# One zero region of the value-cache gradient: from one SyncE store to two GpSimd stores of eight rows

## The chip, the cores and the metric

The kernel runs on one core of a Trainium2 chip. A core has five engines that work side by side: TensorE (PE, and PEld for its weight loads), VectorE (DVE), ScalarE (ACT), GpSimd (POOL) and SyncE (SP), which here only issues transfers. Transfers between the device memory and the core's on-chip memory are carried out by 16 DMA engines that the issuing engines share. The metric is the device time of one execution in microseconds.

## The reference

The reference is the forward pass and the gradients of one decode step of a transformer block: attention over the last part of a key and value cache, beside a gated feed-forward layer, both on the normalised input.

```python
W = min(4096, max(256, Sk // 4))                    # Sk = 4096, so W = 1024
k = jnp.repeat(k_cache[:, :, Sk - W:, :], rep, axis=1)
v = jnp.repeat(v_cache[:, :, Sk - W:, :], rep, axis=1)
scores = jnp.einsum("bhqd,bhkd->bhqk", q, k) * (Dh ** -0.5)
p = _softmax(scores, axis=-1)
o = jnp.einsum("bhqk,bhkd->bhqd", p, v)
...
return x + _A_ref(xn, A_k_cache, A_v_cache, A_wq, A_wo) + _B_ref(xn, B_w_gate, B_w_up, B_w_down)
...
_out, _vjp = jax.vjp(_f, A_x, A_k_cache, A_v_cache, A_wq, A_wo, B_w_gate, B_w_up, B_w_down)
```

The batch is 4, with one query position each, a model width of 512, 32 query heads on 8 key heads of 128, and a hidden width of 1792. All tensors are bfloat16. Nine outputs are returned: the result and eight gradients. The gradients of the two caches have the caches' full shape, 4 x 8 x 4096 x 128. Only the last 1024 positions of each head were used, so the first 3072 positions of both gradients are zero, and the kernel has to write these zeros: 2 caches x 4 x 8 x 3072 x 128 x 2 bytes, which is most of what it stores.

## The kernel before

The program goes through four stages. First the weights are loaded and the feed-forward layer is computed with its gradients. Then follows the preparation of the attention (queries, and the gradient of the attention's output through `wo`). Then there is a loop over the four batch rows, in which each turn computes the scores, the softmax and its gradient, and the gradients of the used part of the two caches, four stores of 1 MB per turn. The last phase computes the gradients of `wo` and `wq` (eight results of 1 MB) and the two small outputs.

Large results are copied from the accumulators into a stage of four buffers (`stg`) and stored from there by SyncE. The engines' orders, GpSimd's apart, are as written. Loads and stores go through SyncE's queue in program order, with the exception of one small input.

The zeros are written from one tile, `ztile` (L215 to L217), whose partitions hold 6144 zeros (12 KB) each. A zero region is two heads' 3072 positions of one batch row of one cache gradient. There are 32 regions of 1536 KB, listed in `ztodo` (L265). `zeros(n)` (L273) takes the next n of them and has SyncE store each one from 64 of the tile's partitions, every second one, in pieces of 12 KB. `zsrc` is that source pattern: 64 rows, each read twice. With `deep=4`, a zero store waits until the fourth one before it has landed.

When the zeros go out is written by hand. `result()` stores a finished result, and before it takes as many zero regions as the list `before` (L105) has for that result. Further zeros follow some loads (`zeros(2)`, `zeros(3)` and others). In the last phase the list was `[2] + [1] * 7`: two regions ahead of the first of the eight weight-gradient results, then one ahead of each.

Around the change, GpSimd clears tiles: `dhs` (L394) in the feed-forward stage, then `bd`, `selh` and `dqs` (L443 to L450) in the preparation. In the loop it copies columns into `bd` (`refill`, L520). It issues no transfer. `wo` is loaded by SyncE at L302, the last of the weight loads. The head of the last phase is at L779 to L785, after the sum `s_o`; there, the last three pieces of the last cache-gradient results (`last`) have still to leave the accumulators in program order, and the latest zero region taken is the third of those ahead of the two previous results.

Of the kernel before, what the change touches and what calls it, by code (L numbers as in the profile page):

```python
# [19 lines left out]
def kernel(  # L20
# [24 lines left out]
    nc = tc.nc  # L45
# [7 lines left out]
    K0 = Sk - W  # L53
# [4 lines left out]
    KH = HD // P  # L58
# [43 lines left out]
    def stg_tile():  # L102
        return stage.tile([P, 4096], BF16, name="stg", tag="stg")

    before = deque([0, 0, 0, 1, 1, 1] + [0, 0, 1, 0] + [0, 0, 2, 0] + [0, 0, 2, 0] + [3, 0, 2, 0] + [2] + [1] * 7)  # L105

    def result(out, in_):
        zeros(min(before.popleft(), len(ztodo)))
# [106 lines left out]
    ZW = K0 // ZP * Dh  # L215
    ztile = const.tile([P, ZW], BF16, name="ztile")
# [32 lines left out]
    wo_sb = wres.tile([P, KH, D], BF16, name="wo_sb")  # L249
# [15 lines left out]
    zsrc = bass.AP(tensor=ztile.tensor, offset=ztile.offset, ap=[[2 * ztile[:].ap[0][0], ZP], [0, ZG], [1, ZW]])  # L265
    ztodo = [(og, b, g) for b in range(B) for g in range(0, G, ZG) for og in (out_2, out_3)]
    zdone = []

    def behind(ins, other):
        tc.add_manual_dep(ins, other.name,  # L270
                          mybir.DependencyInfo(mybir.DependencyClass.Sync, mybir.DependencyReason.DATA))
# [13 lines left out]
    if True:  # L285
# [13 lines left out]
        nc.sync.dma_start(out=wu_sb[:].rearrange("p c f -> p (c f)"), in_=B_w_up.rearrange("(p c) f -> p (c f)", c=C))  # L299
        nc.sync.dma_start(out=wd_sb[:].rearrange("p c n -> p (c n)"), in_=B_w_down.rearrange("(p c) n -> p (c n)", c=FB))  # L300
        nc.sync.dma_start(out=wq_sb[:].rearrange("p c n -> p (c n)"), in_=A_wq.rearrange("(p c) n -> p (c n)", c=C))
        nc.sync.dma_start(out=wo_sb[:].rearrange("p k n -> p (k n)"), in_=A_wo.rearrange("(p k) n -> p (k n)", k=KH))  # L302

        for wsb, t_ in ((wg_sb, hg), (wu_sb, hu)):
            ps = bank("h_ps", "w", (P, FQ))
# [116 lines left out]
    with tc.tile_pool(name="mid", bufs=1, reuse_waits="tile") as mid:  # L422
# [4 lines left out]
        with (tc.tile_pool(name="kvp", bufs=1, reuse_waits="tile") as kvp,  # L427
# [7 lines left out]
            D3 = [att.tile([P, B, DPB, Q], U32, name=n) for n in ("D3q", "D3d")]  # L435
            qm = att.tile([P, B, 4, Dh], BF16, name="qm")
            rows = [qm[:], dyBD[:].rearrange("p n r x -> p (n r x)").rearrange("p (b g d) -> p b g d", b=B, g=4)]
            bd = []
            for k in range(2):
                bd.append([])  # L440
# [120 lines left out]
            def small(name, shape=(P, 1)):  # L561
                return att.tile(list(shape), FP32, name=name, tag=name)
# [77 lines left out]
            for b in range(B):  # L640
                S = sps[0][:]
                m = small("m")
# [136 lines left out]
            s_o = sums[:, 0:D]  # L779
            TT(out=s_o, in0=ob_ps[:], in1=fo[:], op=ALU.add)  # L780

            dwo_v = out_5.rearrange("(p t k) n -> t p (k n)", t=4, k=8)
            dwq_v = out_4.rearrange("(p c) j -> c p j", c=C)
            late = {}
# [126 lines left out]
```

## Time and profile before

| what | value |
|---|---|
| median of 3 runs | 276.7 us (276.59 to 276.91) |
| the profiled execution | 276.85 us |
| its span, first to last instruction | 275.1 us |
| bytes moved | 111.88 MB: HBM read 30.68, written 81.01 |
| mean transfer rate | 407 GB/s |
| busy share PE, PEld, DVE, ACT, POOL | 62, 21, 64, 44, 11% |
| chain that ended last, by engine | PE 27, DVE 17, ACT 7, DMA 6, issue 4% |
| zero stores | 32 of 1536 KB, median 18.3 us from issue to landing |
| mean granted TensorE clock | 0.603 |

The profile page cuts the span into 40 slices of 6.9 us. Each digit of its line "DMA" is the mean busy share of the 16 DMA engines in that slice, in tenths, and the line below gives the rate. Other views list the instructions of an engine in order of time ("start, duration, line, operation, output<-input"; the issue of a transfer is counted with its waiting), busy time by stretch, and the chain of waits that ended last. The trace also has each DMA packet's start, duration and size, and the times at which each transfer's completion semaphore was raised. A packet is one piece of a transfer on one DMA engine; the trace doesn't say on which.

### The profile page before, as it was taken

Reading aid. Unit: us, or ns where it says so; the run is one execution under the profiler, and the core shown is the slowest. Engines: PE = TensorE matmul, PEld = TensorE weight load, DVE = VectorE, ACT = ScalarE, POOL = GpSimd, SP = SyncE. Lnnn points to the kernel's source line nnn. Section 1 sums busy time; section 2 is a strip of 40 time slices with the busy share of each in tenths; the row PEclk is TensorE's granted clock in tenths of the full one; section 3 lists DMA queues with packets and bytes.
Section 4 is the critical chain, followed back from the end, with each engine's and each line's share of the span. In section 5 each row is a group of like instructions: output and inputs, shape, how many; then the busy total and the mean of one; then the engine's idle time right before and its main releaser. Section 6 shows DMA issues by size and latency. Waiting matters only on the chain.

```text
span 275.1 us, 3144 instructions
## 1 busy us (share of the span) xinstructions
PE 171.7 (62%) x1095; PEld 57.4 (21%) x1095; DVE 175.8 (64%) x332; ACT 122.1 (44%) x246; POOL 30.7 (11%) x91
## 2 busy tenths in 40 slices
PE   1257988878247668937788778987979956200000
PEld 0121341123023212313223322341112311000000
DVE  7879669988887497515784498619996688300000
ACT  2343674940202766543675556647574455300000
POOL 8500005251152011200000000000000000000000
PEclk9985885558855955555555555555595575555555
DMA  7999989999999999999999999999999999999993
GB/s 267 435 472 401 434 338 421 429 423 403 425 403 436 407 415 415 409 412 402 406 408 433 400 417 417 429 406 431 418 420 407 417 416 429 423 424 421 421 426 152
DMA packets 24432, 111.88 MB, mean 407 GB/s; under 512 B 1361, under 2 KB 1377, under 8 KB 18785
## 3 DMA queue, kind: packets, MB, share of 16 engines
q1 hardware_dynamic: 24408, 111.69, 99.5%
q8 instruction: 8, 0.13, 0.2%
q14 instruction: 8, 0.06, 0.0%
q10 hardware_dynamic: 8, 0.00, 0.0%
HBM read 30.68 MB, written 81.01 MB: 406 GB/s over the span
## 4 chain that ended last, share of the span: by engine, by line
PE 27%; DVE 17%; ACT 7%; DMA 6%; issue 4%; DVEq 0%; ACTq 0%
DVE scr L94 8%; DMA out_dram<-stg 6%; PE kv_ps L131 5%; PE dw_ps L131 4%; PE od_ps L131 4%; PE sc_ps L131 3%; ACT stg L114 2%; PE ok_ps L131 2%; DVE dqs L728 2%; DVE stg L114 2%; ACT late L114 2%; PE dxq_ps L131 1%; DVE wq_t L94 1%; PE dn_ps L131 1%; PE ob_ps L131 1%
## 5 line engine op out<-in xcount | busy, mean ns | idle before, releaser
L114 ACT CAST stg<-kv_ps 128x512 bf16<-128x512 f32 x102 | 54.6, 601 | 41.0 <-PE kv_ps L131 34.1
L131 PE MATMUL sc_ps<-scr,bd 128*32 128x256 bf16 x256 | 19.6, 399 | 17.1 <-DVE scr L94 16.7
L131 PE MATMUL kv_ps<-qm,spr 64*128 64x512 bf16 x64 | 24.3, 582 | 2.2 <-DVE stg L114 0.8
L131 PE MATMUL kv_ps<-dyBD,spr 64*128 64x512 bf16 x64 | 20.7, 584 | 3.4 <-ACT stg L114 3.3
L94 DVE STREAM_TRANSPOSE scr<-va 128x1024 uint32<-128x1024 uint32 x16 | 19.5, 1224 | 0.0
L114 DVE CAST stg<-kv_ps 128x512 bf16<-128x512 f32 x10 | 6.6, 689 | 16.0 <-PE kv_ps L131 16.0
L131 PEld LDWEIGHTS <-spr 64*128 64x128 bf16 (+1 forms) x192 | 9.2, 106 | 29.4 <-issue 25.0
L612 DVE SCALAR_TENSOR_TENSOR odt<-od_ps,om,odt 128x128 f32<-128x128 f32 x12 | 4.2, 351 | 15.6 <-ACT odt L607 15.4
L131 PEld LDWEIGHTS <-bd 128*32 128x32 bf16 x256 | 6.3, 106 | 34.2 <-issue 33.4
L89 ACT CAST stg<-dwg_ps 128x448 bf16<-128x448 f32 x26 | 11.9, 571 | 3.0 <-DVE scr L94 1.9
L114 DVE CAST stg<-dw_ps 128x512 bf16<-128x512 f32 x16 | 10.5, 685 | 4.2 <-PE dw_ps L131 4.0
L131 PE MATMUL dw_ps<-scr,xn_b 32*128 32x512 bf16 x32 | 9.6, 546 | 5.7 <-ACT late L114 4.0
L114 ACT CAST late<-dw_ps 128x512 bf16<-128x512 f32 x16 | 9.2, 587 | 8.5 <-PE dw_ps L131 8.5
L131 PE MATMUL do_ps<-scr,dyBD 128*128 128x512 bf16 x32 | 10.6, 472 | 2.4 <-DVE scr L94 2.3
L114 DVE CAST late<-dw_ps 128x512 bf16<-128x512 f32 x16 | 10.6, 678 | 1.8 <-PE dw_ps L131 1.7
L114 ACT CAST stg<-dw_ps 128x512 bf16<-128x512 f32 x16 | 8.9, 588 | 5.9 <-PE dw_ps L131 5.3
L94 DVE STREAM_TRANSPOSE scr<-wo_sb 128x1024 uint32<-128x1024 uint32 x8 | 9.7, 1230 | 1.3 <-ACT scr L465 0.7
L94 DVE STREAM_TRANSPOSE scr<-ka 128x1024 uint32<-128x1024 uint32 x8 | 9.8, 1234 | 0.8 <-PE r_ps L131 0.7
L94 DVE STREAM_TRANSPOSE scr<-kb 128x1024 uint32<-128x1024 uint32 x8 | 9.9, 1240 | 0.1
L520 POOL COPY bd<-D3d 32x64 bf16<-32x64 bf16 x32 | 7.0, 231 | 23.7 <-DVE D3d L94 11.4
L520 POOL COPY bd<-D3q 32x64 bf16<-32x64 bf16 x32 | 7.2, 239 | 19.6 <-PE sc_ps L131 15.9
L131 PE MATMUL dw_ps<-dy_b,scr 32*128 32x512 bf16 x32 | 8.5, 528 | 1.0 <-ACT late L114 0.7
(200 smaller groups left out, 314.7 us busy)
## 6 DMA issues: line engine op xcount, KB each, us to landing
out_dram<-ztile SPq DMA_DIRECT2D x32, 1536.0 KB, 18.3
out_dram<-stg SPq DMA_DIRECT2D x18, 1024.0 KB, 16.2
va<-in_A_v_cache_dram SPq DMA_DIRECT2D x8, 1024.0 KB, 12.9
out_dram<-stg SPq DMA_DIRECT2D x6, 896.0 KB, 8.5
wq_sb<-in_A_wq_dram SPq DMA_DIRECT2D x1, 4096.0 KB
wo_sb<-in_A_wo_dram SPq DMA_DIRECT2D x1, 4096.0 KB
ka<-in_A_k_cache_dram SPq DMA_DIRECT2D x4, 1024.0 KB, 12.7
kb<-in_A_k_cache_dram SPq DMA_DIRECT2D x4, 1024.0 KB, 15.6
```

The source lines that it names most:

```text
L89: return nc.scalar.copy(out=out, in_=in_)
L94: nc.vector.transpose(out=out, in_=in_)
L114: return nc.scalar.copy(out=out, in_=in_) if eng == "act" else nc.vector.tensor_copy(out=out, in_=in_)
L131: nc.tensor.matmul(out, lhsT=lhsT, rhs=rhs, start=first, stop=last, **kw)
L520: nc.gpsimd.tensor_copy(out=t_[q, :, :, g2, :, o_:o_ + 4], in_=src[q, b, g2])
L612: STT(out=t_[:], in0=ps[:, g, :], scalar=(om, oms)[k][:, g:g + 1], in1=t_[:], op0=ALU.mult, op1=ALU.add)
L728: nc.vector.tensor_copy(out=dqs[q, :, :, :, a * B + b], in_=d3v[q])
```

## The change

One of the 32 zero regions, the last of the list, is taken out of `ztodo`: heads 6 and 7 of batch row 3 of the value cache's gradient. SyncE no longer stores it, and the list `before` has one region ahead of each of the eight last results. GpSimd stores it in two halves, one head each. Each half has 8 rows with 8 pieces of 12 KB: the source is eight partitions of `ztile` (0, 2, ... 14), each read eight times, and the target's 3072 positions are cut into 8 x 8 runs of 48.

The first half stands in the program ahead of GpSimd's clearing of `bd` and waits until the load of `wo` has landed. The second stands at the head of the last phase and waits for the zero store that SyncE took last before that place.

```diff
-    before = deque([0, 0, 0, 1, 1, 1] + [0, 0, 1, 0] + [0, 0, 2, 0] + [0, 0, 2, 0] + [3, 0, 2, 0] + [2] + [1] * 7)
+    before = deque([0, 0, 0, 1, 1, 1] + [0, 0, 1, 0] + [0, 0, 2, 0] + [0, 0, 2, 0] + [3, 0, 2, 0] + [1] * 8)
...
     zdone = []
+    zog, zb, zg = ztodo.pop()
+
+    def half_zeros(h, after):
+
+        z = nc.gpsimd.dma_start(
+            out=zog[zb, zg + h, 0:K0, :].rearrange("(m i j) d -> m i (j d)", m=8, i=8),
+            in_=bass.AP(tensor=ztile.tensor, offset=ztile.offset, ap=[[2 * ztile[:].ap[0][0], 8], [0, 8], [1, ZW]]))
+        behind(z.ins, after.ins)
...
-        nc.sync.dma_start(out=wo_sb[:].rearrange("p k n -> p (k n)"), in_=A_wo.rearrange("(p k) n -> p (k n)", k=KH))
+        wo_d = nc.sync.dma_start(out=wo_sb[:].rearrange("p k n -> p (k n)"),
+                                 in_=A_wo.rearrange("(p k) n -> p (k n)", k=KH))
...
+            half_zeros(0, wo_d)
             bd = []
...
             TT(out=s_o, in0=ob_ps[:], in1=fo[:], op=ALU.add)
 
+            half_zeros(1, zdone[-1])
             dwo_v = out_5.rearrange("(p t k) n -> t p (k n)", t=4, k=8)
```

## The prediction

> **What bounds the kernel now.** I read the transfer lines of the page first, since every one of their slices is full:
>
> ```profile
> DMA  7999989999999999999999999999999999999993
> GB/s 267 435 472 401 434 338 421 429 423 403 425 403 436 407 415 415 409 412 402 406 408 433 400 417 417 429 406 431 418 420 407 417 416 429 423 424 421 421 426 152
> ...
> q1 hardware_dynamic: 24408, 111.69, 99.5%
> ```
>
> The 16 DMA engines are busy from the first slice to the last, and nearly all of it is one queue, SyncE's (q1). Then I asked for busy time by stretch; the columns are PE, weight loads, DVE, ACT, POOL, granted clock, DMA share (overlapping packets can put it above 1) and GB/s:
>
> ```profile
> 60.00:104.00 44.00, 28.58 (x213) 11.00 (x213) 34.27 (x60) 13.58 (x29) 10.90 (x51) 0.69 1.02 415
> 122.00:204.00 82.00, 66.75 (x414) 22.77 (x415) 56.91 (x108) 49.75 (x109) 0.00 (x0) 0.52 1.03 415
> 236.00:275.00 39.00, 0.00 (x0) 0.00 (x0) 0.45 (x1) 0.39 (x1) 0.00 (x0) 0.50 0.90 377
> ```
>
> Arithmetic is over at 236 us, and for another 39 us only transfers run. The issues on SyncE's queue (start, duration with its waiting) say how that backlog is fed:
>
> ```profile
> 177.17 9.34 SPq L277 DMA_DIRECT2D out_dram<-ztile  x3
> 192.42 1.83 SPq L109 DMA_DIRECT2D out_dram<-stg  x2
> 194.30 8.09 SPq L277 DMA_DIRECT2D out_dram<-ztile  x2
> 204.50 1.79 SPq L109 DMA_DIRECT2D out_dram<-last  x2
> 206.34 7.38 SPq L277 DMA_DIRECT2D out_dram<-ztile  x2
> 213.82 1.31 SPq L109 DMA_DIRECT2D out_dram<-late  x1
> ...
> 251.27 1.32 SPq L109 DMA_DIRECT2D out_dram<-stg  x1
> ```
>
> The last store is issued at 251.3 and lands at 274.3, behind a queue of some 15 to 20 us. So the time is the work of the busiest DMA engine plus the ends. The trace keeps the landing events of each transfer, one for each engine that worked on it, 16 for a full one. Two things follow from them.
>
> First, no engine runs dry. The first landings of successive transfers follow each other by their service time: 3.64 to 3.8 us for a zero store, about 2.6 for 1 MB in 2 KB pieces, 2.5 for 1 MB in 8 KB pieces. When a later transfer is issued, the fastest engine still has at least 4.2 us of queued work (at 33.9); further low points are 4.3 (41.2), 4.7 (89.1), 5.3 (134.0) and 5.5 (192.4).
>
> Second, the engines are unequal. The last store lands at 269.19 on the fastest, by 270.40 on nine, and at 271.96 to 274.26 on the other seven. The 5 us between them grow from 0.9 us at the start. Only the identity of engines 0 to 3 can be read, from the four-row result stores (four landings, besides one at issue): "scr" lands at 245.03, 245.19, 247.45 and 249.64, just behind a full store that landed between 244.40 and 249.47. So of the first four engines two are early, and one is the last or within 0.02 us of it.
>
> **The change, part by part.** The sum goes against the profiled execution: span 275.1 us, time 276.85, which is 0.15 over the median of 276.7.
>
> *Removed*: one SyncE zero store of 1536 KB (1.573 MB), out of the pair at 206.34. On each of 16 engines it is 8 packets of 12 KB at 460 ns (packet records; median) = 3.68 us. The `[1] * 8` list does only this; the other 31 stores keep order and places.
>
> *Added*: the same bytes as two stores of 64 pieces of 12 KB. Nothing is saved in bytes, so the gain in engine work is 0 on average. What matters is which engines carry it. If each half is dealt by its eight rows to eight engines, each of these gets 8 pieces x 460 ns = 3.68 us, what every engine had before. Two complementary sets of eight make the sum per engine exactly the old one: -3.68 + 3.68 = 0. The same set twice makes -3.68 + 7.36 = +3.68 us on eight engines. The trace has no store from GpSimd, so its set is unknown; ends -3.0 (the halves go to early engines only, and the end falls to the mean landing, 271.25, of the last store) and +3.68. I take 0, because a four-row transfer here does use exactly as many engines as rows, and nothing in the trace lets a second transfer find the first one's engines preferred.
>
> [...]
>
> *GpSimd's own time*: two issues, not in the trace. Low end SyncE's shortest, 0.26 us, high end its median zero issue, 1.33 us with waiting; I take 1 us, and it is hidden:
>
> ```profile
> 8.88 1.74 POOL L394 MEMSET dhs<- 128x896 bf16 x2
> 43.98 3.63 POOL L443 MEMSET bd<- 128x1024 bf16 x4 [33.36 <-DVE scr L94]
> ...
> 112.82 1.08 POOL L520 COPY bd<-D3d 32x64 bf16<-32x64 bf16 x4 [1.76 <-PE sc_ps L131]
> ```
>
> GpSimd idles from 10.6 to 43.98. The first half adds a wait for wo's load, whose last landing is at 37.78; behind it stand the four bd memsets, which wait until 43.98 anyway, so 6.2 us of cover are left. Beyond that, their readers are the copies into bd, the next idle time is 11.4 us before 74.18, and then TensorE's scores. The second half waits for the zero store issued at 185.16 (landed 197.92 to 203.05; it is the last one issued in program order before the head of the last phase, where three matmul results of "last" are still out). Nothing stands behind it on GpSimd, whose last copy ends at 113.9. Cost 0.
>
> *SyncE's queue*: one issue less, before the first "late" store at 213.82; that store comes some microseconds sooner into a queue that holds 9 us or more from there on. Worth 0.
>
> *Order of work on the engines*: this is what really moves. From about 38 us until after 203 us one set of eight engines is 3.68 us behind the other. Landings count when the last engine is done, so everything on SyncE lands up to 3.68 us later in that time. Who waits for landings is in the chain:
>
> ```profile
> 103.63 0.28 PE kv_ps L131
> 103.91 17.04 DMA out_dram<-stg
> 120.95 0.02 issue
> ...
> 121.02 1.08 ACT stg L114 x2
> ```
>
> ScalarE waits at 113.5 to 121 for two stage buffers (landed 118.43 and 120.95). This wait grows by up to 3.68 us; from there to 236 the chain is arithmetic, all of which moves by as much. It is hidden as long as the transfers have a backlog. On the eight engines without the first half, the low points of the backlog fall to 5.3 - 3.7 = 1.6 us (134.0) and 1.8 us (192.4). The first issue of the kernel starts at 0.80 and its packets at 1.82, so an issue needs about 1.0 us: no hole, but only 0.6 us from one. The points before 113.5 stay, as no engine waits for a landing there. The loads of keys and values have more: va's last landing at 73.33 is read from 79.87 on. I cost it at 0, with an upper end of 1.5 us where the cover is gone.
>
> The sum: -3.68 + 3.68 + 0 + 0 = 0: 276.9 us, own range 276.3 to 277.5.
>
> **Rivals.**
>
> *Both halves on the same eight engines, slower.* Its place is the end of the kernel. If engines 0 to 7 carry both, the slowest of the first four ends 3.68 us later: 276.85 + 3.68 = 280.5. It decides as soon as the second set has engine 0, 1, 2 or 3 again with the late one among them. For it: a source of eight rows at one end of ztile, and no mechanism in sight that remembers. Against it: nothing in the trace. Chance 0.18.
>
> *Eight neighbouring source rows feed slower, slower.* The zero stores of today read 64 rows spread over all 128 partitions, and each packet runs at 12288 B / 460 ns = 26.7 GB/s, as do all large packets. The halves read partitions 0, 2, ... 14 alone, with eight engines at once. If two engines had to share what one gets now, a piece takes 920 ns and each half costs its engines 3.68 us more: at most 280.5; if the other queue's packets fill part of that, half, 278.7. For it: no row shows so narrow a source. Against it: 26.7 GB/s looks like the engine's own limit, since pieces of 7, 12, 14 and 32 KB all reach 26.4 to 27.0. Chance 0.12. [...]
>
> *The stagger drains the leading half, slower.* The mechanism is the longer wait for stage buffers above, with the backlog at 134 or 192 us falling under 1 us. Each dry spell costs up to 1 us; on the nine early engines 4 us or more are free, but at least five of the seven late engines are outside the first four. 277.5 to 278.4, say 277.9. Chance 0.14.
>
> *The stagger helps, faster.* After 36 us some packets take longer than their kind's usual time (packet records: 24 us summed over 16 engines, 1.5 us each, mostly 2 KB pieces of cache loads, and the packets beside them, and 12 KB zeros). If half of the engines load while the others store, up to half of that, 0.8 us, could go: 276.1; a little rebalancing of unequal engines would add to it. Against it: loads already run on the early engines while the late engines still store, and there (126 to 132 us) the long packets are thickest. Chance 0.18.
>
> **How the numbers follow.** Forecast 0.38; rivals 0.18, 0.12, 0.14 and 0.18. A difference of 0.2%, 0.55 us, is about what a measurement of this kernel can tell from none. Of the forecast 0.31 lies within it, 0.04 below and 0.03 above; of the draining rival 0.02 within. Faster: 0.18 + 0.04 = 0.22. Same: 0.33. Slower: 0.18 + 0.12 + 0.12 + 0.03 = 0.45. The range reaches from 275.8 (the helping stagger and a little rebalancing) to 280.6 (the two dear rivals), leaving out under 0.1 on each side.
>
> **What would show it.** Right: a second queue of some 1.57 MB with two issues on GpSimd near 38 and 203 to 208 us; landings of full transfers spread by about 3.7 us more from 40 to 205 us, and by the old 5.1 us at the end; the last store landing near 274; DMA share of the slices still 9. The same set twice would show as a spread that does not fall back, near 8.8 us. Crowded source rows would show as 12 KB packets near 900 ns. A dry leading half would show as a gap between first landings longer than the service time. The prediction is wrong if the end moves without the spread of the last store moving.

## The result and the profile after

The changed kernel takes 284.48 us, the median of 4 runs (284.21 to 285.05), beside 276.64 for the kernel before in the same session. The ratio is 1.0284, with a 95% interval of 1.0267 to 1.0302: 7.8 us slower. The prediction was 276.9 with a range up to 280.6. The profiled execution took 284.53 us, with a span of 282.8.

The page of the changed kernel, its transfer lines:

```profile
DMA  7999999999999999999999999999999999999984
GB/s 277 440 434 441 375 393 367 421 424 406 412 402 423 408 398 412 420 407 414 399 407 429 394 423 415 432 407 436 406 426 267 220 389 428 426 420 427 423 370 205
...
q1 hardware_dynamic: 24264, 110.12, 96.1%
q0 software_dynamic: 288, 1.57, 3.2%
```

A slice is now 7.07 us. The line "DMA" reads as before, full from end to end, and it hides the whole result. The line below it tells it: the 31st and 32nd slice (212 to 226 us) move 267 and 220 GB/s where their neighbours move 389 to 428. The new queue q0 carries 1.57 of 111.7 MB, 1.4% of the bytes, but its packets take 3.2% of the engines' time.

GpSimd's and SyncE's instructions in order of time (start, duration, line; of the changed kernel):

```profile
38.85 0.76 POOL L272 DMA_DIRECT2D out_dram<-ztile  x1 [28.21 <-DMA wo_sb<-in_A_wo_dram]
42.69 3.62 POOL L453 MEMSET bd<- 128x1024 bf16 x4 [3.07 <-DVE scr L94]
...
207.76 0.55 POOL L272 DMA_DIRECT2D out_dram<-ztile  x1 [93.13 <-DMA out_dram<-ztile]
```

```profile
59.05 11.21 SPq L285 DMA_DIRECT2D out_dram<-ztile  x2
...
210.44 8.29 SPq L285 DMA_DIRECT2D out_dram<-ztile  x1
218.84 3.62 SPq L109 DMA_DIRECT2D out_dram<-late  x1
...
259.09 1.32 SPq L109 DMA_DIRECT2D out_dram<-stg  x1
```

The two GpSimd stores begin where they were put, and the memsets of `bd` wait for VectorE, not for them. Right behind the second store, SyncE's issues take longer (3.62 us for the first "late" store, 1.31 in the kernel before); its last store is issued at 259.1 instead of 251.3.

Busy time by stretch, columns as in the prediction. First the changed kernel, then the kernel before:

```profile
42.00:52.00 10.00, 8.17 (x54) 1.76 (x48) 9.47 (x16) 6.93 (x15) 3.77 (x5) 0.50 1.03 378
214.00:221.00 7.00, 7.00 (x63) 1.46 (x62) 4.15 (x7) 3.51 (x6) 0.00 (x0) 0.50 1.01 235
221.00:228.00 7.00, 6.16 (x31) 2.39 (x29) 4.62 (x11) 3.27 (x7) 0.00 (x0) 0.50 0.94 240
```

```profile
42.00:52.00 10.00, 8.13 (x55) 1.79 (x52) 9.45 (x15) 6.25 (x15) 3.78 (x5) 0.50 1.04 424
214.00:221.00 7.00, 6.73 (x46) 2.41 (x39) 4.43 (x9) 3.03 (x7) 0.00 (x0) 0.54 1.04 415
221.00:228.00 7.00, 3.52 (x13) 0.96 (x13) 6.86 (x17) 4.40 (x8) 0.00 (x0) 0.70 1.01 423
```

The DMA share (second from last) stays at 1.01 and 0.94, while the rate falls from 415 and 423 GB/s to 235 and 240. In these 14 us (415 - 235) x 7 + (423 - 240) x 7 = 2.54 MB less are moved, which at the 415 GB/s of the long middle stretch is 6.1 us. In the first half's stretch, 42 to 52 us, the rate is 378 instead of 424: 0.46 MB, 1.1 us. Together 7.2 of the 7.8 us.

The packet records say which packets it is. Of the first half, all 64 pieces fall between 42.8 and 49.5 us; the median is 460 ns as usual, but 24 of them take over 600 ns (936, later up to 1872). Of the second half (212.9 to 227.7 us) 63 of 64 take over 600 ns, with a median of 1684 and a maximum of 1909. Beside them 35 of SyncE's 145 zero packets in 212 to 226 us take 898 to 975 ns, with a median of 929, and 113 of its 2 KB packets take 140 to 180 instead of 84. At 12288 B, 929 ns is 13.2 GB/s, half of an engine's 26.7. Of the second half's pieces 40 take 1650 ns or more, with a median of 1733, which is 7.1 GB/s, about a quarter. One packet at 13.2 and two at 7.1 make 27.4 GB/s together, close to one engine's 26.7. That one SyncE packet and two GpSimd pieces share what one engine moves is an estimate from these three figures: which packets ran against each other the trace doesn't say.

The chain that ended last, at the place that the prediction watched:

```profile
108.21 16.74 DMA out_dram<-stg
124.95 0.02 issue
...
125.03 1.07 ACT stg L114 x2
```

ScalarE's wait for stage buffers ends at 124.95 instead of 120.95. The later loss is not there: it is in the stretch from 212 to 228 us.

The landings of the last store: four engines between 271.4 and 274.8, four between 278.8 and 280.2, and eight between 281.1 and 281.9; before, all sixteen were between 269.19 and 274.26. The four-row store "scr", which has four landings, lands at 254.17, 254.23, 254.93 and 257.22, behind a full store that has four landings up to 250.39, four from 253.98 to 255.66 and eight from 256.48. Of its four engines (the prediction's engines 0 to 3; the trace doesn't number them) three land with the middle group and one with the last. That is 7.5 to 9.1 us later than before, though the runs with one half alone (below) point to these four as carriers of the first half, not of the second; the earliest engine of the last store is only 2.2 us later (271.4 for 269.19). SyncE's slowed packets are the likely place: what they take over their usual times sums to 25.8 us in 212 to 226 us, which would be 6.5 us each on four engines. The trace doesn't name their engines, so this is not shown.

### The profile page after: what moved, and what is told of

It reads as the page before. It is cut to its first block, busy times and chain, and to the rows that moved or that the text cites. A ratio compares the mean times of both kernels' runs of the same rounds, so it can differ in the third digit from the quotient of the medians.

```text
span 282.8 us, 3144 instructions
## 1 busy us (share of the span) xinstructions
PE 175.0 (62%) x1093; PEld 58.0 (20%) x1095; DVE 176.5 (62%) x332; ACT 121.7 (43%) x246; POOL 32.2 (11%) x93
## 3 DMA queue, kind: packets, MB, share of 16 engines
q0 software_dynamic: 288, 1.57, 3.2%
## 4 chain that ended last, share of the span: by engine, by line
PE 30%; DVE 16%; ACT 6%; DMA 6%; issue 3%; DVEq 0%; ACTq 0%
PE kv_ps L131 7%; DVE scr L94 7%; DMA out_dram<-stg 6%; PE dw_ps L131 5%; PE od_ps L131 5%; PE sc_ps L131 3%; PE ok_ps L131 3%; DVE stg L114 2%; ACT stg L114 2%; DVE dqs L738 2%; ACT late L114 2%; PE dxq_ps L131 1%; PE ob_ps L131 1%; PE dn_ps L131 1%; DVE wq_t L94 1%
## 5 line engine op out<-in xcount | busy, mean ns | idle before, releaser
L131 PE MATMUL kv_ps<-qm,spr 64*128 64x512 bf16 x64 | 25.0, 601 | 2.1 <-DVE stg L114 0.8
L131 PE MATMUL kv_ps<-dyBD,spr 64*128 64x512 bf16 x64 | 21.6, 611 | 6.6 <-ACT stg L114 6.6
L272 POOL DMA_DIRECT2D out_dram<-ztile x2 | 1.3, 656 | 121.3 <-DMA out_dram<-ztile 93.1
L114 DVE CAST stg<-dw_ps 128x512 bf16<-128x512 f32 x16 | 10.6, 686 | 4.5 <-PE dw_ps L131 4.3
L131 PE MATMUL do_ps<-scr,dyBD 128*128 128x512 bf16 x31 | 9.8, 434 | 2.7 <-DVE scr L94 2.3
L131 PE MATMUL dw_ps<-dy_b,scr 32*128 32x512 bf16 x32 | 9.2, 575 | 1.0 <-ACT late L114 0.7
```

Source lines behind the costliest of these rows:

```text
L114: return nc.scalar.copy(out=out, in_=in_) if eng == "act" else nc.vector.tensor_copy(out=out, in_=in_)
L131: nc.tensor.matmul(out, lhsT=lhsT, rhs=rhs, start=first, stop=last, **kw)
L272: z = nc.gpsimd.dma_start(out=zog[zb, zg + h, 0:K0, :].rearrange("(m i j) d -> m i (j d)", m=8, i=8), in_=bass.AP(tensor=ztile.tensor, off ...
```

## The experiments

The leading theory: a piece's rate is set by the group of partitions that it is read from, and eight rows 0 to 14 load a few such groups far too heavily. The rivals: GpSimd's queue itself is expensive; the lag of one set of engines against the other costs; the eight engines carry both halves.

### The rows that are read

*Same stores, other source rows.* The first half reads partitions 0, 4, ... 28, the second 64, 68, ... 92. The order, the queues and the sizes stay.

```diff
-            in_=bass.AP(tensor=ztile.tensor, offset=ztile.offset, ap=[[2 * ztile[:].ap[0][0], 8], [0, 8], [1, ZW]]))
+            in_=bass.AP(tensor=ztile.tensor, offset=ztile.offset + 64 * h * ztile[:].ap[0][0],
+                        ap=[[4 * ztile[:].ap[0][0], 8], [0, 8], [1, ZW]]))
```

> The changed kernel with other source partitions alone: the first half reads every fourth partition from 0 to 28, the second every fourth from 64 to 92; targets, queue, times and the eight rows stay. Theory A (crowded source: eight pieces at a time from sixteen neighbouring partitions come out slower as soon as other stores read on-chip memory too): no 12 KB packet of GpSimd's queue beyond about 600 ns, the 14 us at about 238 GB/s around the second half go back to about 420, and the time falls to 277 to 279; what is left over 276.7 is the price of the lag between the two sets of engines. Theory B (the lag itself starves the leading eight engines): most of the 7.8 us stay, 281 or more. Theory C (transfers issued by GpSimd are dear in themselves, or the targets are): unchanged, about 284.

Measured: 275.81 us, ratio 0.9972 (0.9961 to 0.9983). This is below the 277 to 279 of theory A: not only is the loss gone, this version is ahead of both kernels. Three of the 128 pieces still take over 600 ns, up to 825. Its page and its stretches:

```profile
q1 hardware_dynamic: 24264, 110.12, 98.3%
q0 software_dynamic: 288, 1.57, 1.4%
```

```profile
42.00:52.00 10.00, 8.18 (x54) 1.76 (x48) 9.48 (x16) 6.93 (x15) 3.77 (x5) 0.50 1.04 426
214.00:221.00 7.00, 6.80 (x57) 1.62 (x56) 4.76 (x9) 3.88 (x7) 0.00 (x0) 0.50 1.02 391
221.00:228.00 7.00, 5.47 (x30) 2.26 (x29) 5.15 (x12) 3.91 (x8) 0.00 (x0) 0.74 1.03 426
```

The same 288 packets of q0 now take 1.4% of the engines' time, their share of the bytes, and the rates are back. GpSimd's queue, the count of eight engines and a lag of one set (its size is given below) are all still there, so none of them is the cause of the loss.

*Sixteen rows of 4 pieces each*, from partitions 0, 8, ... 120:

```diff
-            out=zog[zb, zg + h, 0:K0, :].rearrange("(m i j) d -> m i (j d)", m=8, i=8),
-            in_=bass.AP(tensor=ztile.tensor, offset=ztile.offset, ap=[[2 * ztile[:].ap[0][0], 8], [0, 8], [1, ZW]]))
+            out=zog[zb, zg + h, 0:K0, :].rearrange("(m i j) d -> m i (j d)", m=16, i=4),
+            in_=bass.AP(tensor=ztile.tensor, offset=ztile.offset, ap=[[8 * ztile[:].ap[0][0], 16], [0, 4], [1, ZW]]))
```

> Each half has 16 rows of 4 pieces instead of 8 rows of 8, read from every eighth partition of the whole tile, so that every DMA engine takes part. Theory A: no crowding, 276.3 to 277.3. Theory B: no lag, the same 276.3 to 277.3. Theory C: still dear, 280 or more. If this lands at 277 and the run with the spread eight rows at 278 to 279, the difference is the price of the lag.

Measured: 278.90, ratio 1.0089 (1.0068 to 1.011). This lies between what theories A and C expected. Twice as many rows, spread over all 128 partitions, and yet 2.5 us slower than the kernel before: neither the number of rows nor their spread decides alone.

*Eight rows as far apart as eight rows can be*, 0, 16, ... 112:

```diff
-            in_=bass.AP(tensor=ztile.tensor, offset=ztile.offset, ap=[[2 * ztile[:].ap[0][0], 8], [0, 8], [1, ZW]]))
+            in_=bass.AP(tensor=ztile.tensor, offset=ztile.offset, ap=[[16 * ztile[:].ap[0][0], 8], [0, 8], [1, ZW]]))
```

> The changed kernel with source partitions 0, 16, 32, ... 112 for both halves, so the eight rows lie as far apart as eight rows can. If the loss comes from rows that are neighbours, this is as good as the spread source of the first run, 275.5 to 276.5. [...]

Measured: 287.08, ratio 1.0396 (1.0358 to 1.0435), slower than the neighbouring rows of the change (284.48) and 10.6 us above the 275.5 to 276.5 that was expected if nearness is what costs. Stretches of this kernel:

```profile
42.00:52.00 10.00, 8.17 (x54) 1.76 (x47) 9.48 (x16) 6.34 (x15) 3.77 (x5) 0.50 1.01 330
214.00:221.00 7.00, 7.00 (x61) 1.45 (x60) 4.59 (x7) 3.19 (x6) 0.00 (x0) 0.50 1.04 310
221.00:228.00 7.00, 6.80 (x48) 2.51 (x47) 4.67 (x9) 3.38 (x7) 0.00 (x0) 0.59 0.99 295
```

Of the first half 31 pieces take over 600 ns, of the second all 64, with a median of 1066; the first half suffers more than in the change (330 against 378 GB/s). So "neighbouring" was the wrong word: rows 16 apart get in each other's way (287.08 us), and the rows 4 apart of the first experiment, within 32 partitions, do not (275.81). That partitions fall into fixed groups is the author's reading; the runs don't show which belong together. Why the time is 2.6 us above that of the change stays open, since all pieces together take 138.0 us here and 144.5 there.

In order of time, the source rows are 0, 4, ... 28 with 64, 68, ... 92 in the second half (275.81 us), 0, 4, ... 28 for both halves (278.71, next run), 0, 8, ... 120 (278.90), 0, 2, ... 14 (284.48) and 0, 16, ... 112 (287.08).

*The second half on the same eight rows as the first*, 0, 4, ... 28 for both:

```diff
-            in_=bass.AP(tensor=ztile.tensor, offset=ztile.offset, ap=[[2 * ztile[:].ap[0][0], 8], [0, 8], [1, ZW]]))
+            in_=bass.AP(tensor=ztile.tensor, offset=ztile.offset, ap=[[4 * ztile[:].ap[0][0], 8], [0, 8], [1, ZW]]))
```

> As the run with the spread source, but the second half too reads partitions 0, 4, ... 28. [...] If only the crowding of the eight among themselves mattered, 275.5 to 276.2 as in the spread run.

Measured: 278.71, ratio 1.0075 (1.0054 to 1.0096). This is (1.0075 - 0.9972) x 276.7 = 2.8 us over the version that reads 64, 68, ... 92 in the second half, and all that differs is 64 partitions of offset. The second half's pieces have a median of 857 ns, and 53 of 64 take over 600, and the rate falls where they run:

```profile
214.00:221.00 7.00, 6.58 (x42) 2.42 (x39) 4.46 (x9) 3.05 (x7) 0.00 (x0) 0.55 0.97 268
```

A piece at 857 ns has 14.3 GB/s, near half of 26.7. In the first half the same rows cost nothing: no piece there takes over 502 ns. So what a set of rows costs differs from one half to the other. The halves run beside other transfers and, by the landings, on different engines; the trace doesn't name a packet's engine, and which of the two it is was not shown.

*The kernel before, with SyncE's own stores reading rows 0 to 63* instead of every second one. GpSimd stores nothing here:

```diff
-    zsrc = bass.AP(tensor=ztile.tensor, offset=ztile.offset, ap=[[2 * ztile[:].ap[0][0], ZP], [0, ZG], [1, ZW]])
+    zsrc = bass.AP(tensor=ztile.tensor, offset=ztile.offset, ap=[[ztile[:].ap[0][0], ZP], [0, ZG], [1, ZW]])
```

> The kernel before, with all 32 zero stores of SyncE read from partitions 0 to 63 instead of every second one of 128; nothing goes through GpSimd. If a group of eight partitions gives one engine's rate and no more, each zero store takes 7.3 us instead of 3.7 and the time goes to some 350 to 395. If it gives two engines' rate as long as its counterpart in the other half of the tile is not read (the first half of the change ran eight engines at 460 ns a piece from sixteen partitions while the others loaded), the stores run at nearly full rate: 277 to 290. If the source plays no part, 276.6.

Measured, in one run: 408.96 us, 132 us over the kernel before and above every range that was expected. Its page:

```profile
span 407.3 us, 3144 instructions
...
DMA  8999999999999999699999999999999999999962
GB/s 327 449 432 359 386 231 246 269 264 229 319 208 311 341 309 284 222 284 387 238 294 317 227 288 214 298 206 255 257 268 235 244 247 265 253 247 270 257 178 70
...
out_dram<-ztile SPq DMA_DIRECT2D x32, 1536.0 KB, 28.5
```

3004 of the 4096 zero packets take over 600 ns, with a median of 962. The DMA share is full in nearly every slice, mostly at 200 to 320 GB/s. So it isn't GpSimd's queue: SyncE's own stores slow too when they read rows 0 to 63 (962 ns where 460 is usual). The stride of 2 in `zsrc`, which looks like an accident of layout, is worth 132 us.

### Which half costs what

*Only the second half crowded* (first 0, 4, ... 28; second 0, 2, ... 14), and *only the first half crowded* (first 0, 2, ... 14; second 64, 68, ... 92):

```diff
-            in_=bass.AP(tensor=ztile.tensor, offset=ztile.offset, ap=[[2 * ztile[:].ap[0][0], 8], [0, 8], [1, ZW]]))
+            in_=bass.AP(tensor=ztile.tensor, offset=ztile.offset,
+                        ap=[[(4, 2)[h] * ztile[:].ap[0][0], 8], [0, 8], [1, ZW]]))
```

```diff
-            in_=bass.AP(tensor=ztile.tensor, offset=ztile.offset, ap=[[2 * ztile[:].ap[0][0], 8], [0, 8], [1, ZW]]))
+            in_=bass.AP(tensor=ztile.tensor, offset=ztile.offset + 64 * h * ztile[:].ap[0][0],
+                        ap=[[(2, 4)[h] * ztile[:].ap[0][0], 8], [0, 8], [1, ZW]]))
```

> The first half from the spread rows (0, 4, ... 28), the second as in the change (0, 2, ... 14): the loss of the second half with the lag still made good. Its pieces took 101 us in sum in the changed kernel, 71.5 more than at 460 ns, which is 8.9 us on each of its eight engines; the second half alone, on the other set, lost 5.9. If the crowding of the second half is nearly all of the loss, 281.5 to 284. If half of it is the leading engines running dry behind the first half, 279 to 281.

> The first half as in the change (0, 2, ... 14), the second from the spread rows of the other side (64, 68, ... 92). The first half's pieces took 14 us more in sum than at 460 ns, 1.75 on each engine. If that alone counts, the lag is 5.4 us and the time 275.8 + 1.75 = 277.5, or less where the late engines of the other set hide it. If a lag of 5.4 us also makes the leading engines run dry (in the changed kernel the eight of them landed within 0.2 us of each other at 79 us, as engines do that wait for an issue), 278 to 280.

Measured: 282.78, ratio 1.0213 (1.0186 to 1.024), and 277.46, ratio 1.002 (1.0005 to 1.0035). The stretches, first with only the second half crowded, then with only the first:

```profile
42.00:52.00 10.00, 8.17 (x54) 1.76 (x47) 9.48 (x16) 6.34 (x15) 3.77 (x5) 0.50 1.03 421
214.00:221.00 7.00, 6.80 (x52) 1.95 (x50) 4.74 (x8) 3.42 (x6) 0.00 (x0) 0.50 1.01 222
```

```profile
42.00:52.00 10.00, 8.15 (x54) 1.78 (x52) 9.46 (x16) 6.54 (x15) 3.77 (x5) 0.50 1.02 379
214.00:221.00 7.00, 7.00 (x63) 1.56 (x62) 4.16 (x7) 3.52 (x6) 0.00 (x0) 0.50 1.00 387
```

The rate falls where the crowded half is, and only there. Against the version with neither crowded (0.9972), the second half costs (1.0213 - 0.9972) x 276.7 = 6.7 us and the first (1.002 - 0.9972) x 276.7 = 1.3. Their sum, 8.0, stands beside (1.0284 - 0.9972) x 276.7 = 8.6 for both, the same within the intervals. The packet records of the change give the sizes: the first half's 64 pieces sum to 43.5 us where 64 x 460 ns are 29.4, so 14.1 / 8 = 1.8 us on each of its engines; the second half's sum to 101.0, so 71.6 / 8 = 8.9 us. The kernel loses somewhat less, which leaves room for engines that were early.

*One half by GpSimd, the other by SyncE* from 64 rows as usual, first the first half alone, then the second alone:

```diff
+    def half_sync(h):
+
+        nc.sync.dma_start(
+            out=zog[zb, zg + h, 0:K0, :].rearrange("(m j) d -> m (j d)", m=ZP),
+            in_=bass.AP(tensor=ztile.tensor, offset=ztile.offset, ap=[[2 * ztile[:].ap[0][0], ZP], [1, ZW]]))
...
-            half_zeros(1, zdone[-1])
+            half_sync(1)
```

```diff
-            half_zeros(0, wo_d)
+            half_sync(0)
```

> The first half as in the change; the second is stored by SyncE from 64 rows at the head of the last phase. Theory A: the first half met only cache loads for most of its time and its pieces were slow only at the end (about 1.8 us on its engines), so the low-rate stretch at 214 to 228 us is gone; eight engines stay behind by half a region more than before: 278 to 280.5. Theory B: the lag of the first set now lasts to the end, 280 or more, about what the full change costs. Theory C: half of the 7.8 us, 280.5.

> The first half is stored by SyncE from 64 rows in its place; the second as in the change. Theory A: the crowding meets the stores of the last phase as in the change, so most of the loss stays: a stretch of 10 us or more at 300 GB/s or less after 205 us, 280 to 284. As the only transfer from GpSimd it may take the other eight engines; then the first four, told by the small four-row stores, are among the last to finish. Theory B: no lag before 205 us, so at most 1 to 4 us: 277.5 to 280.5. Theory C: half, 280.5.

Measured: 279.09, ratio 1.0084 (1.0062 to 1.0105), and 282.46, ratio 1.021 (1.0187 to 1.0233). The second place is again the dear one. Each number also holds an imbalance that the other runs don't have (the eight engines of the GpSimd half end up with 1.84 us more work than before and the other eight with 1.84 us less), so these two show the order, and the pair before shows the prices. They also tell which engines get a GpSimd store: with the second half alone, eight engines land the last store near 274.1 and the rest up to 280.5, and "scr" lands at 250.1, 251.2, 252.0 and 255.9, among the late. With the first half alone, "scr" too lands among the late eight, at 248.1 to 250.5. In both runs GpSimd's only eight-row store went to the set with the four engines of "scr".

The loss with the second half alone is of another make than in the change. On the same rows and at the same place, its pieces take 874 ns at the median and 55.3 us in sum; as GpSimd's second store, in the run with only the second half crowded, they take 1705 ns and 105.3 us. The first store goes to one set of eight engines and the second to the other, so the set may be what differs; this was not shown by itself. The 874 ns pieces make (55.3 - 29.4) / 8 = 3.2 us on each of their engines, which with the 1.84 is about 5 of the 5.8 us lost. Here the leading engines also ran dry, and the DMA share is 0.88, where the change has 1.01 in this stretch:

```profile
208.25 15.04 SPq L291 DMA_DIRECT2D out_dram<-ztile  x1
214.00:221.00 7.00, 6.80 (x56) 1.53 (x55) 4.66 (x9) 3.72 (x7) 0.00 (x0) 0.50 0.88 273
```

SyncE's issue takes 15 us, and its store lands on the leading eight engines between 228.18 and 228.29, over 10 us after the store before it (218.07 on the first), where 3.65 is usual.

### The lag alone

*No lag*: each half is cut into two stores of 8 rows with 4 pieces, one from 0, 4, ... 28 and one from 64, 68, ... 92, both at the same place:

```diff
-        z = nc.gpsimd.dma_start(
-            out=zog[zb, zg + h, 0:K0, :].rearrange("(m i j) d -> m i (j d)", m=8, i=8),
-            in_=bass.AP(tensor=ztile.tensor, offset=ztile.offset, ap=[[2 * ztile[:].ap[0][0], 8], [0, 8], [1, ZW]]))
-        behind(z.ins, after.ins)
+        for s in range(2):
+            z = nc.gpsimd.dma_start(
+                out=zog[zb, zg + h, s * K0 // 2:(s + 1) * K0 // 2, :].rearrange("(m i j) d -> m i (j d)", m=8, i=4),
+                in_=bass.AP(tensor=ztile.tensor, offset=ztile.offset + 64 * s * ztile[:].ap[0][0],
+                            ap=[[4 * ztile[:].ap[0][0], 8], [0, 4], [1, ZW]]))
+            behind(z.ins, after.ins)
```

> Each half is cut into two stores of eight rows with four pieces, one from partitions 0 to 28 and one from 64 to 92, issued together: the good source, but all sixteen engines at the same time, so no set lags. If the 0.8 us that the spread source gained over the kernel before come from the lag (loads of one set beside stores of the other: its long packets fell from 1.5 to 0.9 us an engine), this is 276.3 to 277. If they come from GpSimd's queue beside SyncE's, or from the place of the stores, it is 275.5 to 276.

Measured: 276.85, ratio 0.9999 (0.999 to 1.0008). The move of the region to GpSimd's queue costs nothing and brings nothing; what the first experiment gains, (0.9999 - 0.9972) x 276.7 = 0.7 us, comes with the lag of one set of engines. The packet records say where it could go: the excess over each kind's usual time, for packets more than 20 ns over it after 36 us, sums to 1.52 us per engine in the kernel before, 1.30 without the lag and 0.91 with it. That these shorter packets are the cause fits in sign and size, but was not tried by itself.

## Why the prediction was wrong

**The step that failed is the price in the sum's added term, 8 pieces x 460 ns = 3.68 us.** The bytes and the engines were right: with neither half crowded and no lag, the ratio is 0.9999; in the change, a store behind the first half lands on eight engines at 59.22 to 59.64 us and on the other eight at 64.68 to 67.00; and with the uncrowded rows and the lag the last store lands within 4.2 us. So the halves go to complementary sets of eight engines, as taken; the rival with the same set twice (280.5) did not occur. But the 460 ns came from stores that read 64 rows over the whole tile. In the change the term measured 43.5 / 8 = 5.4 us on each engine of the first half and 101.0 / 8 = 12.6 us on each of the second, and SyncE's packets beside the second half, which the sum left alone, took 25.8 us in sum over their usual times.

**GpSimd's own time at 0: right.** The issues took 0.76 and 0.55 us, less than the 1 us taken. The memsets of `bd` began at 42.69 (before: 43.98) and waited for VectorE.

**The rival "Eight neighbouring source rows feed slower" named the cause, the rows that are read, but its price was too low, and so was the chance of 0.12 that it got.** The bound of 280.5 came from two engines sharing what one has now: 920 ns for a piece. The pieces of the second half took 1684 ns at the median and up to 1909, which is 7.3 GB/s at the median, about a quarter of 26.7; the halves lasted 6.7 us (42.8 to 49.5) and 14.8, where 8 x 920 ns make 7.4. The bound also counted the halves' own engines alone, whereas 35 of SyncE's 145 zero packets beside them took some 929 ns, and engines that seem to carry none of the second half ended late too. The argument against it, that 26.7 GB/s "looks like the engine's own limit", was true of what the rows showed, and said nothing of a narrow source, which no row of before had. "Neighbouring" was wrong as well, as the run with rows 16 apart shows.

**The lag, hidden: half right.** Landings spread by 7.8 us at 57 to 60 us in the change, 4.5 with the uncrowded rows and 2.0 before; the prediction had 3.7 more, not 5.8 more. So the crowded first half made the lag larger. In the change the leading eight engines landed a zero store within 0.11 us of each other at 74.5 us, which looks as if they had waited for its issue, and its first landing came 4.28 us after that of the load before it, instead of 3.66 in the kernel before. The backlog had been counted from the start of an issue; but of the pair at 59.05 the first one lasted 10.56 us (before: 6.6) and ended only 0.5 us before the leading engines had done what they had. What this costs is small, as the crowding of the first half, with the larger lag that it brings, costs 1.3 us.

**The helping stagger, 276.1, chance 0.18: this is what the change would have done with rows that don't collide.** The price of 0.8 us was met: 276.61 - 275.81.

**What would show it.** "12 KB packets near 900 ns" was there to be seen, and so was the spread of the last store, 10.5 us instead of 5.1. "DMA share of the slices still 9" came true and told nothing.

## What to carry to other kernels

A store that reads few partitions has to be priced by which partitions these are and by what runs beside it, not by its bytes or its own engines alone: here eight rows in place of eight others make 8.6 us. Look at GB/s beside the DMA share: here a share of 1.01 at 235 GB/s, where the kernel before has 1.04 at 415, went with pieces of 1684 ns. When one region is moved to a second queue, try several sets of source rows, and a different set for each store (here 0, 4, ... 28 first and then 64, 68, ... 92, 275.81 us, beside 278.71 with 0, 4, ... 28 for both); the small lag between the engines may even be a gain, 0.7 us here.

## What was not expected of the hardware

- The slow packets are not all slowed alike beside the second half: 929 ns at the median for SyncE's and 1733 ns for the slow GpSimd pieces, about a half and a quarter of 26.7 GB/s. Which packets met was not shown.
- DMA engines whose packets ran slowly counted as busy here. In the run with SyncE's rows 0 to 63, the share was 0.98 at 290 GB/s between 100 and 204 us:

```profile
100.00:204.00 104.00, 53.43 (x361) 19.86 (x359) 39.50 (x83) 38.51 (x83) 3.94 (x16) 0.52 0.98 290
```

- The first four or five pieces per engine of each first half took 460 ns even with crowded rows, in the change and in the runs with sixteen rows and with rows 16 apart. In the change they are 40 pieces of 460 to 592 ns that began from 42.8 to 45.5 us. Why they were spared was not tried and stays open.
- One issue of SyncE's lasted 10.56 us in the change, and one 15.04 us in the run with the second half alone, where the leading engines ran dry. What such an issue waits for was not tried by itself.
